# Two more batches normalized head pair by head pair, and a new order of the work

## The chip, the core and the metric

The kernel runs on one core of a Trainium2 chip. A core has a matrix engine (PE, with its weight loads shown apart as PEld), a vector engine (DVE), a scalar engine (ACT), GpSimd (POOL), and SyncE (SP), which here only issues transfers. The engines run side by side, each through its own list of instructions in order, and wait for each other through semaphores. Matmul results go to PSUM, eight banks of 512 fp32 values in each of 128 partitions; everything else lies in SBUF. The metric is the time of one execution in device microseconds.

## The reference

```python
# q, k, v: (8 batches, 8 heads, 576 tokens, 64)
kv = np.einsum('bhsd,bhse->bhde', k, v)
out = np.einsum('bhsd,bhde->bhse', q, kv)
rms = np.sqrt(np.mean(out * out, axis=-1, keepdims=True) + 1e-06)
attn = out / rms * g_norm                     # then heads side by side: x is (8, 576, 512)
h = np.maximum(x @ w_in, 0.0)                 # w_in 512 x 1024
conv = sum(conv_w[k] * hp[:, k:k + S, :] for k in range(3))   # along tokens, hp is h with a zero row at each end
y = (h * sigmoid(conv)) @ w_out               # w_out 1024 x 512
```

So there is linear attention with a norm over the 64 channels of each head and token, and then a feed-forward layer whose gate is a convolution over three neighbouring tokens. The matmuls run in bf16.

## The kernel before

A token is the smallest unit of a batch's 576 positions. Channels lie across the partitions: two heads of 64 channels make one head pair t, four pairs make the 512 channels. Batches go through the stages one after the other, several at a time, and the feed-forward part works on two batches together (pairs p = 0 to 3).

The steps have short names, and a step with its batch and part is a token of the order below:

- Lq, Lk, Lv, Li, Lo: loads of q, k, v, w_in (four quarters) and w_out, issued on POOL's queue, converted to bf16 on the way.
- kv (L358): the 64 x 64 products of k and v. kvc, kvn, ky: copies of these into SBUF; kx: the same by a transfer.
- qt, qtp (L380, L388): transposes of q on PE, with qc as copies out of PSUM; dq (L436): the same by a transposing transfer for batches 5, 6 and 7.
- ot (L430, L431): attention product of one head pair, for batches 0 to 3, one matmul of 64 columns and one of 512. oq (L464): the same for batches 4 to 7 (QUAD), as four small matmuls on quarters of the array. There the even and the odd tokens' products lie in two banks, 288 columns each, in an order with the token's residue on the outside.
- sq (L493): squares of a product on ACT, bf16, into SBUF, put in natural order of tokens. oc (L341): the product copied on ACT to SBUF as fp32 (o32).
- hm (L640): x times w_in for one slice f of 128 of the 1024 hidden channels, eight matmuls; re (L646 on ACT, L648 on DVE): its relu.
- ta, aa, ab (L682, L683, L689, L695), sg (L728), mg (L734): the convolution as scaled, shifted sums on DVE, the sigmoid on ACT, the gate on DVE. cm (L714) does a few slices of it on PE.
- om (L744): output matmuls for a tile m of 128 tokens, in eight steps or in two groups of four; ea (L341): copy out of PSUM on ACT; st (L778): the store, from SP. oh, eh, sh are the last tile in two halves.
- unread (L427): matmuls on a constant whose results nobody reads.

The squares are summed over the 64 channels of a head in one of two ways:

- In groups (`NORM`, batches 2 to 7). ss (L575) sums a batch's squares by eight matmuls into a row for each head and parity; ln (L584) takes the reciprocal root of these rows, 288 columns; sl (L591 to L594) splits it into bf16 parts on DVE, four instructions; sp (L603) spreads it back over the channels by four matmuls for each half of the tokens; mu (L629) multiplies o32 by g and by the spread factor, for two head pairs at a time. Group 2 holds batches 4 and 5, and batch 6 has group 3. Batch 7 takes its factor through DRAM (L610, L617, L625).
- Directly (batches 0 and 1). on multiplies the squares by a matrix with ones in two 64 x 64 blocks (L430, L431), which gives each channel its head's sum; nl (L542) takes the reciprocal root of 576 columns on ACT; mu0 (L562) multiplies the product, still in PSUM, by g and by the root. sqh, onh, nlh and muh (L535) are halves of these, used once.

What sets the order is a string, ORDER (lines 67 to 121 of the file): a list of tokens, written by a planner beforehand. The kernel runs through it and emits each token's instructions, and a chain of dependencies keeps each engine in the order of emission. "@n" gives a token the PSUM bank (two for a product or an hm) or the buffer of a ring, and ":1" moves a step that ACT or DVE can do to the other of the two. Thus PSUM is allocated by the string too: a step that takes a bank waits until the bank's last reader is done.

Of the kernel before, what the change touches and what calls it, by code (L numbers as in the profile page):

```python
# [54 lines left out]
AL = mybir.AluOpType  # L55
PSUM = bass.MemoryType.PSUM

NORM = {8: [2], 1: [3], 2: [4, 5], 3: [6], 4: [7]}
SPLIT = (0, 3)
QD = (5, 6, 7)  # L60
QP = (4,)
# [3 lines left out]


ORDER = """
pre@0,0,0 unread.10@0 qt0.0.0@0 ps pn qc0.0.0:1@0 pi ca.k.0 ca.v.0 kv.0.0.1@1 kvc.0.0.1.0:1@0 kvc.0.0.1.1 al.h0@0
ct@2 pg qt0.0.1@3 Lq.1.0@1 qc0.0.1:1 ot.0.0@0 Li.1 pc dg.6:1 sq.0.0@0 Li.3 unread.3@4 kv.0.1.1@3 kvc.0.1.1.0:1
dg.7:1 kvc.0.1.1.1:1 al.h1@1 Lv.1.0@1 al.x0@0 on.0.0@4 nl.0.0@0 mu0.0.0 Lk.1.0@1 Li.0 al.x1@1 unread.1@6 qt0.0.2@2  # L70
ot.0.1@6 sq.0.1@1 Lq.1.2 unread.3@3 kv.0.2.1@3 kvc.0.2.1.0:1 on.0.1@4 qt0.0.3@0 kvc.0.2.1.1:1 qc0.0.2:1@1 nl.0.1@1
mu0.0.1 ot.0.2@2 unread.3@1 kv.0.3.1@1,4 Lv.1.2 sq.0.2@2 qc0.0.3:1 kvc.0.3.1.0:1 kvc.0.3.1.1 on.0.2@6 ot.0.3@4
nl.0.2@2 mu0.0.2 sqh.0.3.0@3 unread.3@0 onh.0.3.0@6 sqh.0.3.1 nlh.0.3.0@3 onh.0.3.1 qt.1.0@2 nlh.0.3.1 qc.1.0:1@2
muh.0.3.0 muh.0.3.1 hm.0.2@6 re.0.2 hm.0.3@4 hm.0.6@6 re.0.3 ta.0.2@0 pl re.0.6 Lk.1.2 ta.0.3 aa.0.1 hm.0.7@4
re.0.7:1 cm.0.6@6 kv.1.0.2@2 kvc.1.0.2.0:1@1 sg.0.6@1 Lq.2.0@0 cm.0.7@4 kvc.1.0.2.1 Lv.2.0@0 ot.1.0@2 sg.0.7
hm.0.1@6 sq.1.0@4 qt.1.1@4 ab.0.1 on.1.0@0 nl.1.0@4 Lk.2.0@0 re.0.1:1 hm.0.0@6 re.0.0 qc.1.1@3 mg.0.3 mu0.1.0
ot.1.1@4 sq.1.1@5 kv.1.2.2@0 ta.0.0@1 kvc.1.2.2.0 kvc.1.2.2.1 on.1.1@2 nl.1.1@5 Li.2 ta.0.1 ot.1.2@0 Lq.3.0@1
ot.1.3@6 Lv.3.0@1 Lk.3.0@1 sq.1.2@6 aa.0.0 sq.1.3@7 mu0.1.1 ab.0.0 unread.1@2 on.1.2@2 nl.1.2@6 on.1.3@4 nl.1.3@7
sg.0.1 sg.0.0 qt.2.1@2 qt.2.0@4 mu0.1.2 mu0.1.3 hm.1.2@0 hm.1.3@6 re.1.2 qc.2.0@4 qc.2.1@0 mg.0.0 ta.1.2@1 hm.1.1@2
hm.1.6@0 re.1.3 kv.2.0.4@6 ta.1.3 aa.1.1 hm.0.5@4 ab.1.1 sg.0.2 re.1.1 sg.0.3 re.1.6 kvc.2.0.4.0@0 sg.1.3  # L80
kvc.2.0.4.1:1 mg.0.1 Lo.0 hm.0.4@0 ot.2.2@6 re.0.5 Lo.1 re.0.4:1 sg.1.2 mg.1.1 ta.0.4@0 ot.2.0@4 sq.2.2@0 sq.2.0@1
ta.0.5 hm.1.7@2 hm.1.4@0 re.1.7 oc.2.2@0 aa.0.2 hm.1.5@2 ot.2.1@6 re.1.4 ta.1.4@1 ab.0.2 oc.2.0@1 Lq.4.0@0 re.1.5
sq.2.1@2 qt.3.1@0 oc.2.1 sg.0.4 sg.0.5 qt.3.0@4 hm.1.0@2 ot.2.3@6 ta.1.5 qc.3.1@1 Lq.5.0@1 unread.3@0 kv.3.0.4@0
qc.3.0@2 aa.1.2 mg.0.2 sq.2.3@3 ss.2@1 kvc.3.0.4.0:1@1 kvc.3.0.4.1:1 oc.2.3 re.1.0 ln.8@0 unread.3@4 ot.3.1@2
ot.3.2@6 ot.3.0@4 ta.1.0@0 ta.1.1 ab.1.2 sq.3.2@4 oc.3.2@2 om.0.0.0@0 om.0.1.0@1 om.0.3.0@6 sq.3.0@5 oc.3.0@3
ot.3.3@4 aa.1.0 sl.8@0 om.0.1.4 sq.3.1@6 ab.1.0 om.0.3.4 oc.3.1 Lk.4.0@0 sq.3.3@7 oc.3.3 sp.2.1@2,4 ea.0.1@0
Lv.4.0@0 ea.0.3@1 mu.2.1.0 dq.5.0@3 ss.3@7 Lv.5.0@1 ln.1@0 om.0.0.4 mu.2.1.1 sp.2.0@6,2 om.0.2.0@1 qtp.4.1@4
mu.2.0.0 sg.1.5 ea.0.0@2 mu.2.0.1 hm.2.7@6 sg.1.4 om.0.2.4 qc.4.1@4 re.2.7 ea.0.2@3 sg.1.0 sg.1.1 sl.1@0 hm.2.2@4
sp.3.0@0,6 mg.1.2 mu.3.0.1 hm.2.5@2 mu.3.0.0 mg.1.0 re.2.2 cm.1.6@6 re.2.5 cm.1.7@0 dq.5.1@0 sg.1.6@1 hm.2.4@2
sg.1.7 sp.3.1@0,6 kv.4.0.4@4 mg.1.3 re.2.4 kvn.4.0.4 qtp.4.0@2 mu.3.1.0 Lk.5.0@1 ky.4.0.4.0 ky.4.0.4.1 mu.3.1.1  # L90
qc.4.0@2 hm.3.4@0 al.x2@0 hm.3.5@6 oq.4.0@2 re.3.4 re.3.5 ta.2.4@0 oq.4.1@0 hm.2.6@4 ta.2.5 sq.4.0@0 oc.4.0@1
hm.3.3@6 hm.3.6@2 re.2.6 sq.4.1@1 re.3.3 Lk.7.0@0 oc.4.1 Lv.7.0@0 hm.3.7@4 hm.3.1@0 re.3.6 aa.2.2 re.3.7 ab.2.2
om.0.6.0@4 hm.3.2@2 sg.2.5 re.3.1 sg.2.4 ta.2.6@1 ta.2.7 Lq.7.0@0 om.0.6.4 oq.4.3@0 oq.4.2@6 kv.5.0.4@5 re.3.2
aa.2.3 ea.0.6@4 Lk.6.0@1 ab.2.3 hm.2.3@2 Lv.6.0@1 sq.4.2@2 om.0.4.0@4 kvn.5.0.4:1 ky.5.0.4.0:1 ky.5.0.4.1:1 sq.4.3@3
oc.4.2@0 oq.5.0@6 oc.4.3 re.2.3 oq.5.1@0 sq.5.0@4 mg.2.2 sq.5.1@5 om.0.8.0@5 om.0.4.4 oc.5.0@3 st.0.0 ss.4@2 oc.5.1
oq.5.3@6 ea.0.4@5 oq.5.2@0 ta.2.2@0 sq.5.3@6 sq.5.2@7 om.0.8.4 ta.2.3 om.0.5.0@4 ss.5 om.0.5.4 ln.2@0 hm.2.0@2
oc.5.2@2 oc.5.3 ea.0.5@6 re.2.0 dq.7.0@1 hm.2.1@0 aa.2.1 ea.0.8@7 ab.2.1 re.2.1 sl.2@0 sp.4.1@6,2 mu.4.1.1 mu.4.1.0
om.0.7.0@4 sp.4.0@0,2 kv.7.0.4@5 mu.4.0.0 om.0.7.4 mu.4.0.1 sg.2.3 sp.5.0@0,6 sg.2.2 kvn.7.0.4:1 ea.0.7@2 mu.5.0.1
hm.3.0@2 mu.5.0.0 kx.7.0.4.0 re.3.0 al.x3@1 hm.4.4@6 al.h2@0 re.4.4 mg.2.1 sp.5.1@4,0 mu.5.1.0 kx.7.0.4.1 mu.5.1.1
hm.4.3@2 hm.4.2@6 ta.2.0@0 sg.2.7 hm.5.3@4 sg.2.6 re.4.2 hm.5.2@0 re.5.3 re.4.3 ta.2.1 oq.7.0@6 re.5.2 sq.7.0@0  # L100
oc.7.0@1 kv.6.0.4@4 oq.7.1@0 hm.5.1@2 sq.7.1@1 oc.7.1 mg.2.3 aa.2.0 kvn.6.0.4:1 hm.4.5@6 re.5.1 re.4.5 ab.2.0
hm.5.0@0 sg.2.0 sg.2.1 ta.3.2@1 re.5.0 Lq.6.0@1 ta.3.3 hm.5.5@6 hm.4.7@2 aa.3.1 re.4.7 hm.4.0@4 re.4.0 hm.4.1@0
hm.5.6@4 re.5.5 ab.3.1 mg.2.0 re.4.1 dq.7.1@2 st.0.4 kx.6.0.4.0 hm.5.4@6 om.1.5.0@0 ta.3.0@0 sg.3.2 sg.3.3 st.0.6
st.0.3 re.5.4 oq.7.3@2 re.5.6 oq.7.2@6 sq.7.3@2 kx.6.0.4.1 om.1.8.0@1 dq.6.0@4 dq.6.1@3 ta.3.1 st.0.5 sq.7.2@3
st.0.2 st.0.1 ea.1.5@5 oc.7.2@0 ss.7@4 om.1.4.0@0 hm.5.7@6 ln.4@0 oc.7.3 oq.6.0@2 oq.6.2@4 ea.1.4@4 ea.1.8@1 mg.3.1
sq.6.0@4 fw.4 fr.7.0@0 st.1.4 aa.3.0 re.5.7 oc.6.0@3 ta.3.4@1 sq.6.2@5 om.1.6.0@0 oc.6.2@2 oq.6.3@6 oq.6.1@2
om.1.7.0@1 sq.6.1@6 ta.3.5 ab.3.0 sq.6.3@7 aa.3.2 ab.3.2 ss.6@4 oc.6.3 ln.3@0 sl.3@0 oc.6.1 ea.1.7@6 om.1.0.0@5
om.1.2.0@1 mu.7.0.1 mu.7.0.0 sg.3.0 sg.3.1 sp.6.0@2,6 mu.6.0.0 mu.6.0.1 fr.7.1@1 mg.3.0 om.1.3.0@4 st.0.7 st.1.7
ea.1.2@3 hm.4.6@6 ea.1.3@0 om.1.1.0@4 ea.1.6@4 re.4.6 ea.1.0@2 mu.7.1.0 sp.6.1@6,0 mu.7.1.1 ta.3.6@0 mu.6.1.1 sg.3.5
ta.3.7 al.h3@1 hm.7.3@2 mu.6.1.0 ea.1.1@6 hm.7.7@4 hm.7.6@0 sg.3.4 aa.3.3 hm.6.2@6 re.7.3 re.7.7 hm.6.6@4 re.7.6  # L110
mg.3.2 re.6.2 re.6.6 ab.3.3 hm.6.7@6 re.6.7 hm.7.4@4 hm.7.2@6 hm.6.0@0 sg.3.6 hm.6.3@2 sg.3.7 ta.4.6@1 ta.4.7 re.7.2
re.6.0 st.1.5 st.1.2 hm.6.1@6 re.6.3 re.7.4 re.6.1 st.1.6 aa.4.3 hm.7.1@2 mg.3.3 re.7.1 ab.4.3 sg.4.7 hm.6.4@4
hm.7.5@2 st.1.1 hm.7.0@6 hm.6.5@0 sg.4.6 re.6.4 re.7.0 st.1.3 re.7.5 om.2.4.0@4 re.6.5 om.2.7.0@5 om.2.1.0@0
ta.4.2@0 ta.4.3 om.2.2.0@1 aa.4.1 ea.2.4@5 mg.4.3 ab.4.1 om.2.0.0@4 ta.4.0@1 ta.4.1 sg.4.2 om.2.5.0@2 sg.4.3 aa.4.0
mg.4.1 ab.4.0 ta.4.4@0 ea.2.7@3 ea.2.1@4 ea.2.2@6 ta.4.5 st.2.4 sg.4.1 sg.4.0 st.1.0 st.2.7 st.2.2 aa.4.2 ab.4.2
ea.2.0@0 om.2.3.0@3 ea.2.5@5 om.2.6.0@2 om.2.8.0@4 sg.4.5 mg.4.0 st.0.8 st.2.5 om.3.4.0@5 sg.4.4 mg.4.2 ea.2.6@2
ea.2.3@3 om.3.7.0@3 om.3.4.4 ea.2.8@6 st.2.1 om.3.7.4 om.3.0.0@4 om.3.3.0@2 om.3.0.4 om.3.6.0@1 om.3.5.0@0 om.3.6.4
st.2.6 st.1.8 st.2.8 ea.3.4@7 ea.3.7@5 om.3.5.4 st.2.0 st.3.4 om.3.1.0@3 st.2.3 om.3.3.4 om.3.1.4 om.3.2.0@5
ea.3.0@4 ea.3.6@2 oh.3.8.0@6 ea.3.5@1 ea.3.3@6 om.3.2.4 oh.3.8.1 ea.3.1@0 st.3.5 st.3.7 st.3.6 st.3.0 eh.3.8.0@7
ea.3.2@3 st.3.3 st.3.1 sh.3.8.0 eh.3.8.1 st.3.2 sh.3.8.1  # L120
"""


# [1 line left out]
def kernel(  # L125
# [344 lines left out]
    def product(b, t):  # L470
        ps = T["ot", b, t]
        if b in QUAD:
            return ps[:, :, :HS].rearrange("p e (r n) -> p n r e", n=PS)
        return natural(ps[:, :S])

    def in_order(b, ap):
        if b in QUAD:
            return ap.rearrange("p (n r e) -> p n r e", r=R // 2, e=2)
        return by_r(ap)
# [7 lines left out]
    @op  # L487
    def sq(b, t):
        s = T["sq", b, t] = ring("sq", [P, S], BF16, name="sq")
        if b == 0:  # L490
            nc.scalar.activation(s, T["ot", b, t][:, :S], AX.Square)
        else:
            nc.scalar.activation(in_order(b, s), product(b, t), AX.Square)  # L493
        T["sqi", b, t] = last()

    @op
# [55 lines left out]
    def x_tile(b):  # L552
        return T["x", b // 2][:, :, b % 2, :]

    @op
    def mu0(b, t):
        o, x, r = T["ot", b, t], x_tile(b)[:, t, :], T["rs0", b, t]
        if b:
            o, x, r = product(b, t), in_order(b, x), in_order(b, r)
        else:  # L560
            o = o[:, :S]
        nc.vector.scalar_tensor_tensor(x, o, g_sb, r, op0=AL.mult, op1=AL.mult)  # L562
# [266 lines left out]
```

## Time and profile before

| | |
|---|---|
| time, median of 3 runs | 179.5 us (179.39 to 180.1) |
| profiled execution | 179.07 us, span 177.3 us |
| PE busy | 170.7 us (96%), 1663 matmuls |
| ACT busy | 150.4 us (85%), of it 10 table loads of 1.28 us each |
| DVE busy | 138.4 us (78%) |
| POOL busy | 30.6 us (17%) |
| L640 (hm) | 66.4 us of PE, 512 matmuls |
| L744 (om) | 64.5 us of PE, 280 matmuls |
| L493 (sq) | 28 squares on ACT, 674 ns each |
| L341 (oc) | 24 copies to o32 on ACT, 682 ns each |
| L629 (mu) | 20 multiplications on DVE, 810 ns each |
| granted TensorE clock | full throughout |

The span is the time from the first to the last instruction that the profiler recorded. Busy time counts an instruction from its start to its end, and neighbours overlap, on PE above all, so the busy times of a group can be more than what the group adds to the span. The chain of waits is followed back from the last instruction: at each step to what released it, or else to the instruction before it on its engine; its durations run from start to start and don't overlap. A releaser is inferred from semaphores. In a group's row, "out<-in" gives the operands by the program's names, then partitions x elements, the count, the busy time in us and the mean of one in ns, and last the engine's idle time ahead of the group, with what ended it.

### The profile page before, as it was taken

The page shows a single profiled execution, that of the slowest core. Times are in us where ns is not written, and L with a number is a line of the kernel's source. Part 1 is how long each engine was busy: PE and PEld are TensorE (multiplying, and loading weights), DVE is VectorE, ACT ScalarE, POOL GpSimd, SP SyncE. Part 2 cuts the span into 40 slices and gives each one's busy share as a digit, 9 for nine tenths or more (in the row PEclk, how much of TensorE's full clock was granted, in tenths as well). Part 3 has the DMA queues.
Part 4 walks back from the last instruction along what each step waited for, and adds up shares of the span by engine and source line. Part 5 has one row for each costly group of instructions (what it writes and reads, how often), then busy time and mean ns, then how long its engine had stood idle before and what let it go on. Part 6 is the DMA issues. An engine that isn't in the chain of part 4 may idle for free.

```text
span 177.3 us, 4089 instructions
## 1 busy us (share of the span) xinstructions
PE 170.7 (96%) x1663; PEld 101.8 (57%) x1663; DVE 138.4 (78%) x235; ACT 150.4 (85%) x233; POOL 30.6 (17%) x54
## 2 busy tenths in 40 slices
PE   6999997999999999999999999999999999999993
PEld 2545763877535677653667774434577754444451
DVE  5665779889988968998799999929999999960000
ACT  2479899999999969999999999999989987782342
POOL 7997516100700031050000000000000000000000
PEclk9999999999999999999999999999999999999999
DMA  6999999999999999999995393169430004348075
GB/s 144 198 199 199 200 204 204 203 204 206 205 204 203 197 191 141 190 204 204 189 165 123 117 203 132 33 180 292 153 118 0 4 0 178 122 153 307 14 276 199
DMA packets 36219, 29.49 MB, mean 166 GB/s; under 512 B 8528, under 2 KB 31720, under 8 KB 36200
## 3 DMA queue, kind: packets, MB, share of 16 engines
q0 software_dynamic: 21760, 15.96, 59.2%
q1 hardware_dynamic: 14400, 13.26, 27.4%
q8 instruction: 13, 0.21, 0.5%
q14 instruction: 6, 0.05, 0.1%
q10 hardware_dynamic: 40, 0.01, 0.0%
HBM read 33.70 MB, written 9.58 MB: 244 GB/s over the span
## 4 chain that ended last, share of the span: by engine, by line
PE 76%; DMA 14%; POOL 5%; ACT 2%; issue 1%; POOLq 0%; ACTq 0%
PE bank L744 33%; PE bank L640 30%; DMA w_in_sb<-in_moe_w_in_dram 9%; DMA k_sb<-in_k_dram 5%; PE bank L358 2%; PE bank L464 2%; POOL q_sb L241 1%; PE bank L603 1%; PE bank L575 1%; POOL k_sb L241 1%; POOL v_sb L241 1%; PE bank L759 1%; PE bank L431 1%; PE bank L714 1%; POOL w_in_sb L315 1%
## 5 line engine op out<-in xcount | busy, mean ns | idle before, releaser
L640 PE MATMUL bank<-xT,w_in_sb 128*128 128x288 bf16 x512 | 66.4, 286 | 0.1
L744 PE MATMUL bank<-w_out_sb,h 128*128 128x512 bf16 x280 | 64.5, 379 | 0.0
L640 PEld LDWEIGHTS <-w_in_sb 128*128 128x128 bf16 x512 | 49.1, 98 | 14.7 <-issue 0.6
L744 PEld LDWEIGHTS <-h 128*128 128x128 bf16 x280 | 26.3, 98 | 30.7 <-issue 2.1
L646 ACT ACTIVATE h<-bank 128x576 bf16<-128x576 f32 x61 | 37.9, 657 | 3.1 <-PE bank L640 2.6
L728 ACT ACTIVATE taps<-taps,cwn 128x1152 bf16<-128x1152 bf16 (+1 forms) x36 | 38.0, 1093 | 1.4 <-DVE taps L695 1.3
L341 ACT ACTIVATE row<-bank 128x512 f32<-128x512 f32 (+1 forms) x37 | 21.0, 589 | 11.7 <-PE bank L744 10.0
L734 DVE TENSOR_TENSOR h<-h,taps 128x2304 bf16<-128x2304 bf16 (+1 forms) x20 | 22.3, 1114 | 3.0 <-ACT taps L728 1.8
L689 DVE TENSOR_TENSOR taps<-taps 128x2304 bf16<-128x2304 bf16 (+1 forms) x18 | 20.9, 1160 | 0.4
L695 DVE TENSOR_TENSOR taps<-taps,h 128x2304 bf16<-128x2304 bf16 (+1 forms) x18 | 20.8, 1153 | 0.2
L682 DVE TENSOR_SCALAR taps<-h,cwn 128x1152 bf16<-128x1152 bf16 (+1 forms) x36 | 17.4, 483 | 2.5 <-ACT h L646 2.4
L493 ACT ACTIVATE sq<-bank 128x576 bf16<-128x576 f32 x28 | 17.9, 674 | 0.0
L629 DVE SCALAR_TENSOR_TENSOR xT<-o,cw,bank 128x576 bf16<-128x576 f32 x20 | 15.4, 810 | 2.1 <-PE bank L603 1.9
L683 DVE TENSOR_SCALAR taps<-h,cwn 128x1152 bf16<-128x1152 bf16 (+1 forms) x36 | 16.9, 469 | 0.0
L341 ACT ACTIVATE o<-bank 128x576 f32<-128x576 f32 x24 | 16.0, 682 | 0.0
L213 ACT ACT_TABLE_LOAD x10 | 12.8, 1283 | 2.5 <-issue 2.4
L427 PE MATMUL bank<-fill 128*128 128x512 bf16 x30 | 10.1, 462 | 1.6 <-DVE fill L228 1.5
L301 POOL DMA_DIRECT2D k_sb<-in_k_dram x8 | 6.0, 750 | 26.5 <-PE bank L358 25.7
L301 POOL DMA_DIRECT2D q_sb<-in_q_dram x8 | 6.1, 760 | 17.4 <-PE bank L380 15.1
L358 PEld LDWEIGHTS <-k_sb 96*64 96x64 bf16 x384 | 7.2, 114 | 3.0 <-issue 2.4
L358 PE MATMUL bank<-v_sb,k_sb 96*64 96x64 bf16 x384 | 8.5, 199 | 0.0
L562 DVE SCALAR_TENSOR_TENSOR xT<-bank,cw,root 128x576 bf16<-128x576 f32 x7 | 5.6, 814 | 1.8 <-ACT root L542 1.7
(88 smaller groups left out, 132.0 us busy)
## 6 DMA issues: line engine op xcount, KB each, us to landing
out_dram<-row SPq DMA_DIRECT2D x35, 256.0 KB, 2.6
q_sb<-in_q_dram POOLq DMA_DIRECT2D x6, 576.0 KB, 15.0
v_sb<-in_v_dram POOLq DMA_DIRECT2D x6, 576.0 KB, 14.6
k_sb<-in_k_dram POOLq DMA_DIRECT2D x6, 576.0 KB, 14.8
factor<-factor SPq DMA_DIRECT2D x4, 288.0 KB, 4.8
w_in_sb<-in_moe_w_in_dram POOLq DMA_DIRECT2D x4, 256.0 KB, 8.5
w_out_sb<-in_moe_w_out_dram POOLq DMA_DIRECT2D x2, 512.0 KB, 19.8
q_sb<-in_q_dram POOLq DMA_DIRECT2D x4, 144.0 KB, 4.5
```

The costliest lines, as they stand in the source:

```text
L341: nc.scalar.activation(to, fr, AX.Copy)
L358: nc.tensor.matmul(ps[i][i * D:(i + 1) * D, t - t0, :], k_sb[:, 2 * t + i, r * D:(r + 1) * D], v_sb[:, 2 * t + i, r * D:(r + 1) * D], star ...
L493: nc.scalar.activation(in_order(b, s), product(b, t), AX.Square)
L640: nc.tensor.matmul(ps[:, e, :HS], w_in_sb[:, t, f * P:(f + 1) * P], x[:, t, e * HS:(e + 1) * HS], start=(t == 0), stop=(t == NT - 1))
L646: nc.scalar.activation(to, fr, AX.Relu)
L682: nc.vector.tensor_scalar_mul(tap[:, 0, f % 2, :n, 8:8 + S], h[:, f], cwn[:, 0, f:f + 1])
L683: nc.vector.tensor_scalar_mul(tap[:, 1, f % 2, :n, :S], h[:, f], cwn[:, 2, f:f + 1])
L689: nc.vector.tensor_add(tap[:, 1, :, :n, :S], tap[:, 0, :, :n, 7:7 + S], tap[:, 1, :, :n, 1:1 + S])
L695: nc.vector.tensor_add(y, y, h[:, 2 * j:2 * j + 2])
L728: nc.scalar.activation(y, y, AX.Sigmoid, scale=cwn[:, 1, f:f + 1])
L734: nc.vector.tensor_mul(h, h, T["tap", c, j][:, 1, :, :n, :S])
L744: nc.tensor.matmul(T["om", p, m], h[:, f, m * P:(m + 1) * P], w_out_sb[:, f, :], start=(f == 0), stop=(f == NF - 1))
```

## The change

Batches 5 and 6 leave the groups and are normalized directly. `DIRECT` names the batches that no group holds: 0, 1, 5 and 6.

- Their squares are no longer put in natural order: they are read and written as two contiguous halves by parity.
- on and nl (line numbers shifted) work on these squares as for batches 0 and 1, for each of four head pairs.
- mu0 gets a branch for such batches: two multiplications of 288 columns, one for each parity. The product and the root are read contiguously. The result goes to x in natural order, which means steps of six elements (12 bytes) along the inner loop of 96 and of two elements along the outer loop of three.
- So for each of the two batches ss, the copies oc, the two sp and the four mu are gone, and group 3 with its ln and sl; group 2 keeps batch 4 alone.
- The order is written anew as a whole: 690 tokens for 689. The dummy matmuls are 27 instead of 30, two relus more are done by DVE (five for three), one transposed-q copy of 1152 columns and one small copy move from DVE to ACT, and banks and ring buffers are given out anew.

```diff
-NORM = {8: [2], 1: [3], 2: [4, 5], 3: [6], 4: [7]}
+NORM = {8: [2], 1: [3], 2: [4], 4: [7]}
+DIRECT = [b for b in range(8) if b not in sum(NORM.values(), [])]
...
     def sq(b, t):
...
-            nc.scalar.activation(in_order(b, s), product(b, t), AX.Square)
+            o = product(b, t)
+            if b in DIRECT and b in QUAD:
+                s, o = s.rearrange("p (e n) -> p e n", e=2), T["ot", b, t][:, :, :HS]
+            else:
+                s = in_order(b, s)
+            nc.scalar.activation(s, o, AX.Square)
...
     def mu0(b, t):
+        if b in QUAD:
+            x = x_tile(b)[:, t, :].rearrange("p (n r e) -> p e r n", r=R // 2, e=2)
+            for e in range(2):
+                o, r = (
+                    ap.rearrange("p (r n) -> p r n", n=PS)
+                    for ap in (T["ot", b, t][:, e, :HS], T["rs0", b, t][:, e * HS:(e + 1) * HS]))
+                nc.vector.scalar_tensor_tensor(x[:, e], o, g_sb, r, op0=AL.mult, op1=AL.mult)
+            return
```

Of the order, the stretch around batch 2's sums, before and after, cut to its core (the tokens between that are not spoken of are left out as "..."):

```diff
-... hm.1.0@2 ot.2.3@6 ta.1.5 qc.3.1@1 Lq.5.0@1 unread.3@0 kv.3.0.4@0
-qc.3.0@2 aa.1.2 mg.0.2 sq.2.3@3 ss.2@1 kvc.3.0.4.0:1@1 kvc.3.0.4.1:1 oc.2.3 re.1.0 ln.8@0 unread.3@4 ot.3.1@2
-ot.3.2@6 ot.3.0@4 ... sq.3.2@4 oc.3.2@2 om.0.0.0@0 ... sq.3.0@5 oc.3.0@3
-ot.3.3@4 ... sq.3.3@7 oc.3.3 sp.2.1@2,4
+... hm.1.1@4 ot.2.3@2 ot.2.2@6 sq.2.2@2 sq.2.3@3 re.1.1 oc.2.2@1 mg.0.2 kv.3.0.4@0 ss.2@1 qt.3.0@4 qt.3.1@6
+... oc.2.3 ln.8@0 unread.1@0 ot.3.0@4
+ot.3.1@2 sq.3.0@4 oc.3.0@2 ot.3.2@6 unread.1@0 om.0.1.0@0 ... sq.3.1@5 ... oc.3.1 sq.3.2@6 ot.3.3@2
+... oc.3.2@3 sl.8@0 ... sq.3.3@7 oc.3.3 ea.0.0@0 om.0.1.4 sp.2.1@6,2
```

And the one in which batch 5 is normalized in the new order:

```diff
+oq.5.0@6 oq.5.1@2 sq.5.0@3 ... om.0.4.0@0 ... on.5.0@4 mg.2.2 ab.2.3 om.0.5.4 nl.5.0@4 om.0.4.4
+mu0.5.0 hm.2.3@4 oq.4.1@6 sq.5.1@4 ... om.0.6.0@0 re.2.3 sq.4.1@5 ... on.5.1@4
+ta.2.3 om.0.6.4 oc.4.1 aa.2.1 nl.5.1@7 ss.4@1 oq.5.3@4 ... ea.0.6@4 oq.5.2@6 mu0.5.1 ln.2@0 om.0.7.0@0 sq.5.3@6
+sq.5.2@7 sl.2@0 on.5.3@2 om.0.7.4 nl.5.3@0 mu0.5.3 ea.0.7@6 on.5.2@2 ... nl.5.2@7 om.0.8.0@1
+kv.7.0.4@0 sp.4.0@2,4 mu0.5.2 ...
```

## The prediction

> **What bounds the kernel now.** I read the shares of the page first, then the chain of waits from 36 us on, then busy time by stretch, then the groups of instructions for the prices.
>
> ```profile
> span 177.3 us, 4089 instructions
> PE 170.7 (96%) x1663; PEld 101.8 (57%) x1663; DVE 138.4 (78%) x235; ACT 150.4 (85%) x233; POOL 30.6 (17%) x54
> ```
>
> PE is the bound by share, and ACT is the only other engine near it. The shares are averages, so the chain decides. The columns are start, duration and what the time went to.
>
> ```profile
> 20.48 16.20 DMA w_in_sb<-in_moe_w_in_dram
> 36.69 0.05 issue
> 36.73 2.13 PE bank L640 x16
> ...
> 45.01 0.65 PE bank L427 x3
> 45.66 0.88 PE bank L358 x48
> 46.54 0.36 PE bank L575 x8
> ...
> 48.53 0.50 ACT rs L584
> ...
> 54.07 0.97 PE bank L744 x4
> 55.04 0.23 PE bank L603 x4
> ...
> 57.74 0.86 PE bank L744 x4
> ```
>
> Three things are to be seen. The last quarter of w_in lands at 36.69, and its first matmul starts at once: whatever is gained before that point is waited away. From there the chain is PE almost throughout until 174.2 (ACT holds it only from 48.4 to 51.2). And four output matmuls cost 0.86 when a full-array matmul follows and 0.97 when the small-tile L603 follows: a visit to small tiles (L358, L380, L464, L575, L603) costs about 0.10 on top of its work.
>
> By stretch, the columns are the stretch and its length, then PE, PEld, DVE, ACT and POOL busy:
>
> ```profile
> 36.70:53.30 16.60, 16.50 (x194) 10.00 (x194) 15.20 (x32) 16.57 (x30) 3.85 (x5) 1.00 1.29 205
> 73.00:83.00 10.00, 10.00 (x122) 5.14 (x120) 9.54 (x14) 9.98 (x18) 2.30 (x3) 1.00 1.31 209
> 83.00:93.00 10.00, 10.00 (x122) 5.95 (x122) 8.43 (x14) 9.92 (x15) 0.00 (x0) 1.00 1.20 181
> 93.00:106.00 13.00, 13.00 (x152) 10.18 (x151) 12.93 (x18) 13.00 (x20) 0.00 (x0) 1.00 0.61 142
> 106.00:120.00 14.00, 14.00 (x102) 6.22 (x100) 10.74 (x16) 13.97 (x24) 0.00 (x0) 1.00 0.42 127
> ```
>
> Batch 5 is normalized between 73 and 93 and batch 6 between 106 and 130. ACT has no idle time to speak of in either; only after 140 does it have some (16.2 of 20 us, then 5.5 of 17.3). So PE sets the end, with ACT half a step behind it.
>
> **The prices**, from the groups by shape (busy, mean ns):
>
> ```profile
> L493 ACT ACTIVATE sq<-bank 128x576 bf16<-128x576 f32 x28 | 17.9, 674 | 0.0
> L341 ACT ACTIVATE o<-bank 128x576 f32<-128x576 f32 x24 | 16.0, 682 | 0.0
> L542 ACT ACTIVATE root<-bank,eps_sb 128x576 f32<-128x576 f32 x7 | 5.2, 742 | 0.7 <-PE bank L431 0.5
> L629 DVE SCALAR_TENSOR_TENSOR xT<-o,cw,bank 128x576 bf16<-128x576 f32 x20 | 15.4, 810 | 2.1 <-PE bank L603 1.9
> L562 DVE SCALAR_TENSOR_TENSOR xT<-bank,cw,root 128x576 bf16<-128x576 f32 x7 | 5.6, 814 | 1.8 <-ACT root L542 1.7
> L535 DVE SCALAR_TENSOR_TENSOR xT<-bank,cw,root 128x288 bf16<-128x288 f32 x2 | 0.9, 514 | 0.4 <-ACT root L528 0.4
> ```
>
> Neighbours on a queue overlap: squares and copies follow each other at 0.54 (chain: 49.03, 49.57, 50.11), a root of 576 columns is followed after 0.64 (timeline: 14.15 to 14.79), two multiplications of 576 start 0.73 apart, so one of 288 takes 0.43 to 0.51.
>
> **The change, part by part.**
>
> *PE work after 36.73.* Gone: two L575 groups (0.36 each) and four L603 groups (0.23 each), 1.64 together, and four of the six dummy matmuls that lay there (6 to 2, 0.22 each), 0.86. Added: eight pairs of matmuls with ones, each 0.24 as the product pairs of the same shapes in the chain, 1.94. Net −0.56. Before 36.73 the two batch 1 round trips also get shorter, by about 0.2 by my sums; I count that at nothing, since the loads queued ahead of the last w_in quarter are the same ones in both orders and it should land at 36.7 again. If POOL issued it later, the whole would move one for one.
>
> *Visits to small tiles after 36.73.* Counted in the two orders: 24 before, 18 after, at 0.10 each: −0.6.
>
> *Waits of PE.* Here the new order pays. Just after batch 2's products it has one kv (0.88) and no dummies ahead of ss.2, which needs the last square. From the start of ot.2.2: product 0.24, about 0.2 to the square's start, squares 0.53 and 0.67, release 0.07, so 1.71; PE gets there after 0.24 + 0.88 = 1.12. It waits about 0.6, and the dummies taken out here are no gain. ACT then sets the pace over the squares and copies of batch 3: I sum 1.35 of waits up to sp.2.1, where before had 0.35. So sp.2.1 starts at 53.3 in both, with 0.3 more PE work left in the new order. Later: about 0.2 where sp.3.1 waits for the parts of L591 to L594; about 0.35 in batch 5, mostly at the ones products: on.5.2 takes the bank that nl.5.3 reads, PE covers that with 0.25 + 0.86 = 1.11, the root needs 0.25 + 0.22 + 0.74 + 0.05 = 1.26; 0.2 elsewhere and at the last piece. That is 0.75 against 0.45 before. All waits: 2.1 against 0.8, +1.3.
>
> *ACT.* Eight copies to o32 go (−8 × 0.54 = −4.3), eight roots come (+8 × 0.64 = 5.1), one root of 288 columns goes (−0.4), two relus go to DVE (−1.1), a transposed-q copy of 1152 columns (1.1) and a small copy (0.2) come. Net +0.6 to +0.9 for an engine that was full from 73 to 130. The table loads stay at ten. What covers it is the distance between ACT's results and PE's use of them: by the two orders laid over the row times, results that came up to 3 us ahead in the old order come 0.8 to 1.4 us ahead in the new one. I take it as just covered; uncovered it costs up to 0.9 and more through the round trips (first rival).
>
> *DVE.* Eight L629 (−8 × 0.73 = −5.8) and one set of parts (−1.5) go; sixteen multiplications of 288 (16 × 0.43 = 6.9) and two relus (+1.4) come, 0.9 of copies leave. About zero. It is never on the chain after 36.7. The first users of batch 5's result are matmuls of hm.5.3 far behind; the nearest wait is oq.4.1 for the bank that mu0.5.0 frees: PE has 2.7 us of work there, the trip takes 2.2 (ones 0.25, 0.2 to the root's start, root 0.74, 0.05, two multiplications 0.95).
>
> *The new multiplication's writes.* It reads PSUM and root contiguously and writes bf16 every 12 bytes. No row of before has such a write. Strided reads of PSUM cost nothing (L562 reads strided, 814; L629 does not, 810), so the lower bound is the row, 0.43 to 0.51; as upper bound I take twice the row, as if it made one access per element where L535 makes one per two. I take the row, the nearest; the upper end is a rival. The Trainium skill, "SBUF — State Buffer", Specifications, says that a line holds 16 bytes and that full bandwidth needs two hits per line; 12-byte steps give 1.33, so by that page the writes would be slowed. No run here shows it yet.
>
> *Queues and end.* SP loses nothing and gains nothing in bytes; the q transposes and the stores are reissued in other places, with their first users over 1 us behind. At the end the last piece, its copy (0.38) and its store stay as they were, but two more stores lie in the last 2 us: 0 to +0.3, I take +0.15.
>
> **Sum.** −0.56 − 0.6 + 1.3 + 0.15 = +0.3 us, against an execution whose span was 177.3 and whose time was 179.07, so 1.8 us lie around the span. The median of the runs is 179.5, 0.4 above that execution; the forecast stands on the median: 179.8 us. This kernel's runs spread over 0.7 us, so about 0.5% (0.9 us) is what can be told from no change.
>
> **Rivals.**
>
> *ACT becomes the bound between 73 and 130 us: slower.* Against it: the results still lead by 0.8 us by my sums. For it: the stretches above show ACT at 9.9 to 10 of 10, and ones product and root of one head pair follow its square directly on ACT, so ACT idles for up to a product (0.25 + 0.2) in each of the four trips of batch 5, which the page would show as L542 waiting for L431. It decides once ACT's delay passes 0.8 us. Price: 0.9 more work and four times 0.4 of idle, 2.5, less the 0.8 of lead: +1.7. PE's savings then count for nothing, so it stands on the old median: 181.2.
>
> *The writes at 12-byte steps take double: slower.* Sixteen times 0.43 is 6.9 us more on DVE. In 73 to 93 it had 0.46 + 1.57 idle for 3.5 more, so 1.5 us of delay enter the stretch to 106, where DVE is full (12.93 of 13); batch 6's 3.5 meet 3.3 idle, 0.2 over. If what waits on DVE has no slack, 1.7 reach PE: 179.8 + 1.7 = 181.5. At oq.4.1 the trip would be 3.1 for 2.7. Against it: nothing but the nearest row. By the rule of the Trainium skill given above, on that page of SBUF lines, this would be the outcome.
>
> *PE's waits don't appear: faster.* If ACT runs half a step earlier at ss.2, as it did before (results there were 0.9 ahead), PE keeps −0.56 − 0.6 and the waits stay at 0.8: 179.5 − 1.2 = 178.3. Against it: the wait at ss.2 is a sum of four rows in a fixed order.
>
> **How the numbers follow.** The balance has 0.45 (179.8, own range 178.9 to 180.4), ACT as bound 0.25 (181.2), the slow writes 0.10 (181.5), no waits 0.20 (178.3). Only the last is below 178.6, so faster 0.20; the two slower ones make 0.35; the rest 0.45. The range for 8 in 10 reaches from 178.2, which holds the faster case, to 181.6, which takes in both slow ones at their price and leaves out what is worse.
>
> **What would show it.** After: PE near 170 busy, chain still PE from 36.7; the dummies of L427 (now L428) fall from 30 to 27, the pairs with ones rise by eight; a PE wait of 0.5 or more near 46 us for the squares on ACT; the new multiplication at 0.43 to 0.55 (0.9 or more if the writes are slow). The prediction is wrong if w_in lands away from 36.7, if ACT's idle ahead of the roots of 576 columns passes 1 us in batch 5, or if no PE wait shows near 46.

## The result and the profile after

The changed kernel takes 185.9 us (185.57 to 186.75) for 179.5 before: 1.036 times as long (95% interval 1.0315 to 1.0399), 6.4 us slower. The forecast was 179.8 us with a range up to 181.6. The profiled execution took 186.75 us, the longest of its four, with a span of 185.0. (One execution of a kernel tried below took 594 us, with PE busy for 588 of them; nothing is read from it.)

The page of the changed kernel, its first part:

```profile
span 185.0 us, 4050 instructions
PE 173.7 (94%) x1644; PEld 103.9 (56%) x1644; DVE 146.9 (79%) x239; ACT 151.5 (82%) x232; POOL 31.4 (17%) x54
```

DVE has gained 8.5 us of work where the forecast had none. The groups by shape say where (the multiplication of batches 5 and 6 is L569, the old direct one is L576 now):

```profile
L569 DVE SCALAR_TENSOR_TENSOR xT<-bank,cw,root 128x288 bf16<-128x288 f32 x16 | 16.9, 1225 | 1.6 <-ACT root L548 1.5
L576 DVE SCALAR_TENSOR_TENSOR xT<-bank,cw,root 128x576 bf16<-128x576 f32 x7 | 5.6, 815 | 3.5 <-ACT root L548 3.4
```

Half as many columns take one and a half times as long: 1225 ns for 288 columns, 815 for 576. The nearest row of before, L535, had 514 for the same 288 columns. The chain of waits of the changed kernel, from batch 5 on:

```profile
79.05 1.27 DVE taps L709
80.32 2.05 DVE xT L569 x2
...
85.33 2.06 DVE xT L569 x2
...
88.97 3.99 DVE xT L569 x4
...
93.01 1.02 PE bank L654 x7
...
120.89 2.15 DVE xT L569 x2
...
124.22 2.06 DVE xT L569 x2
```

Before, DVE was never on the chain after 36.7 us. Now it holds it from 75 to 93 and again at 121 and 124, and six pairs of the new multiplication lie on it with 12.3 us. What waits for them is PE, in the view of waits (engine and line, what it waited for, us, times, longest):

```profile
PE bank L465 <- DVE xT L569: 2.2, 4, 0.7
PE bank L654 <- DVE xT L569: 1.4, 2, 0.7
PEld L431 <- DVE xT L569: 1.4, 1, 1.4
PE bank L431 <- DVE xT L569: 0.9, 1, 0.9
```

Products (L465), a hidden slice (L654) and a ones product (L431) wait for a bank whose product the multiplication reads: 4.5 us. The 1.4 us of the weight load (PEld) are the same wait as the 0.9 of L431, seen from the other side, and don't count twice. By stretch, PE then stands idle where it had been full (columns as before: length, then PE, PEld, DVE, ACT, POOL):

```profile
73.00:83.00 10.00, 9.13 (x108) 5.19 (x106) 9.56 (x13) 9.03 (x14) 2.29 (x3) 1.00 1.31 210
83.00:93.00 10.00, 7.75 (x95) 3.34 (x93) 9.86 (x15) 8.28 (x12) 0.00 (x0) 1.00 1.27 212
120.00:140.00 20.00, 18.64 (x115) 10.51 (x114) 18.23 (x21) 16.64 (x24) 0.00 (x0) 1.00 0.54 160
```

### The profile page after: what moved, and what is told of

The parts are those of the page before. It is cut to its first block, busy times and chain, and to the rows that moved or that the text cites. A ratio compares the mean times of both kernels' runs of the same rounds, so it can differ in the third digit from the quotient of the medians.

```text
span 185.0 us, 4050 instructions
## 1 busy us (share of the span) xinstructions
PE 173.7 (94%) x1644; PEld 103.9 (56%) x1644; DVE 146.9 (79%) x239; ACT 151.5 (82%) x232; POOL 31.4 (17%) x54
## 4 chain that ended last, share of the span: by engine, by line
PE 66%; ACT 14%; DVE 12%; DMA 3%; issue 3%; POOLq 0%
PE bank L654 27%; PE bank L758 26%; DVE xT L569 7%; ACT sq L499 3%; ACT taps L742 3%; ACT h L660 3%; DMA q_sb<-in_q_dram 3%; PE bank L359 2%; PE bank L428 2%; ACT o L342 2%; PE bank L728 2%; ACT root L548 2%; PE bank L381 2%; DVE taps L703 1%; PE bank L432 1%
## 5 line engine op out<-in xcount | busy, mean ns | idle before, releaser
L654 PE MATMUL bank<-xT,w_in_sb 128*128 128x288 bf16 x512 | 66.1, 286 | 1.4 <-DVE xT L569 1.4
L654 PEld LDWEIGHTS <-w_in_sb 128*128 128x128 bf16 x512 | 49.2, 98 | 16.2 <-issue 2.6
L660 ACT ACTIVATE h<-bank 128x576 bf16<-128x576 f32 x59 | 37.0, 671 | 2.7 <-PE bank L654 2.5
L748 DVE TENSOR_TENSOR h<-h,taps 128x2304 bf16<-128x2304 bf16 (+1 forms) x20 | 22.2, 1112 | 2.9 <-ACT taps L742 2.3
L696 DVE TENSOR_SCALAR taps<-h,cwn 128x1152 bf16<-128x1152 bf16 (+1 forms) x36 | 16.8, 467 | 2.5 <-ACT h L660 2.5
L569 DVE SCALAR_TENSOR_TENSOR xT<-bank,cw,root 128x288 bf16<-128x288 f32 x16 | 16.9, 1225 | 1.6 <-ACT root L548 1.5
L697 DVE TENSOR_SCALAR taps<-h,cwn 128x1152 bf16<-128x1152 bf16 (+1 forms) x36 | 16.6, 462 | 0.0
L548 ACT ACTIVATE root<-bank,eps_sb 128x576 f32<-128x576 f32 x15 | 11.0, 739 | 4.4 <-PE bank L432 4.3
L342 ACT ACTIVATE o<-bank 128x576 f32<-128x576 f32 x16 | 10.8, 690 | 0.0
L643 DVE SCALAR_TENSOR_TENSOR xT<-o,cw,bank 128x576 bf16<-128x576 f32 x12 | 9.2, 806 | 1.2 <-PE bank L617 1.2
L302 POOL DMA_DIRECT2D k_sb<-in_k_dram x8 | 6.8, 851 | 14.6 <-PE bank L359 13.8
```

Source lines behind the costliest of these rows:

```text
L342: nc.scalar.activation(to, fr, AX.Copy)
L569: nc.vector.scalar_tensor_tensor(x[:, e], o, g_sb, r, op0=AL.mult, op1=AL.mult)
L654: nc.tensor.matmul(ps[:, e, :HS], w_in_sb[:, t, f * P:(f + 1) * P], x[:, t, e * HS:(e + 1) * HS], start=(t == 0), stop=(t == NT - 1))
L660: nc.scalar.activation(to, fr, AX.Relu)
L696: nc.vector.tensor_scalar_mul(tap[:, 0, f % 2, :n, 8:8 + S], h[:, f], cwn[:, 0, f:f + 1])
L697: nc.vector.tensor_scalar_mul(tap[:, 1, f % 2, :n, :S], h[:, f], cwn[:, 2, f:f + 1])
```

## The experiments

Theory 1 was the rival of the prediction: the writes at 12-byte steps. Theory 2 was that the new order is slow by itself, with ACT as the bound.

**The multiplication with other steps.** The first run has the squares in natural order again and one even step of 4 bytes in the write:

```diff
-            o = product(b, t)
-            if b in DIRECT and b in QUAD:
-                s, o = s.rearrange("p (e n) -> p e n", e=2), T["ot", b, t][:, :, :HS]
...
+            nc.scalar.activation(in_order(b, s), product(b, t), AX.Square)
...
-            x = x_tile(b)[:, t, :].rearrange("p (n r e) -> p e r n", r=R // 2, e=2)
+            x = x_tile(b)[:, t, :].rearrange("p (n r e) -> p e n r", r=R // 2, e=2)
+            w = T["rs0", b, t].rearrange("p (n r e) -> p e n r", r=R // 2, e=2)
```

> The changed kernel, with its order, in which squares of batches 5 and 6 go back to natural order (strided read of PSUM, contiguous write) and the two multiplications per head pair write x at one even step of 4 bytes instead of nested steps of 12; root read at 8-byte steps, product strided from PSUM. Theory 1 (the 12-byte writes are the cause): each multiplication takes 0.5 us instead of 1.23, the PE waits at oq.4.1, the last hm and om of that stretch, oq.6.0 and oq.6.1 (6.5 us together) go, time about 179.5 to 180.5. Rival (the new order is slow in itself, ACT the bound): multiplications get fast but PE then waits for ACT roots, time 182 to 185.

The second exchanges the loops alone:

```diff
-            x = x_tile(b)[:, t, :].rearrange("p (n r e) -> p e r n", r=R // 2, e=2)
+            x = x_tile(b)[:, t, :].rearrange("p (n r e) -> p e n r", r=R // 2, e=2)
...
-                    ap.rearrange("p (r n) -> p r n", n=PS)
+                    ap.rearrange("p (r n) -> p n r", n=PS)
```

> The changed kernel with only the two loops of the multiplication exchanged: writes go at 4-byte steps in sequence, but now the fp32 root in SBUF is read at 384-byte steps (and the product in PSUM as well). If only the write's step counts, 0.5 us each and the same time as with the natural order, 179.5 to 180.5. If an SBUF read at far steps costs as the write does, about 1 to 1.2 us each and the time stays at 184 to 186.

Both are 1.0056 times before (intervals 1.0034 to 1.0078 and 1.0031 to 1.0082), 180.5 and 180.7 us. The group and the waits of the second:

```profile
L569 DVE SCALAR_TENSOR_TENSOR xT<-bank,cw,root 128x288 bf16<-128x288 f32 x16 | 8.0, 541 | 3.0 <-ACT root L548 2.9
```

```profile
PEld L431 <- DVE xT L569: 0.4, 1, 0.4
```

The multiplication falls from 1225 to 541 ns with the same operands, engines and order, and PE's waits for it from 4.5 us to none (the 0.4 left is a weight load's, and no matmul waits with it). Some 5.4 of the 6.4 us are the order of two loops (1.0357 against 1.0056 of before).

The changed kernel and this one issue the same 1644 matmuls in the same order, so the starts of the matmuls can be compared one by one. After the first matmul behind w_in the changed kernel falls behind at six places: 1.15 us at oq.4.1, 0.92 at on.5.3, 0.30 at the spread sp.4.0, 1.38 at hm.3.1, 1.11 at oq.6.0 and 0.91 at oq.6.1, 5.8 us together. Nowhere else does one matmul lose more than 0.08.

Where the root is read, at 8-byte or at 384-byte steps, makes no difference (537 and 541 ns). About 1.0 us is left with the order; it is taken up below.

**The steps by themselves.** The kernel before, with a series behind its work:

```diff
+    stt = lambda o, a, c: nc.vector.scalar_tensor_tensor(o, a, g_sb, c, op0=AL.mult, op1=AL.mult)
+    for k in (1, 2, 3, 4, 5, 6, 8, 12):          # elements between writes
+        for _ in range(3):
+            stt(every(bo, k), flat, flat)
...
+            nc.scalar.activation(every(bo, k), flat, AX.Copy)
```

> The kernel before, with a series of 288-column multiplications and ACT copies on dead SBUF buffers added behind its work (their time is in the span and is left out): bf16 written at steps of 2, 4, 6, 8, 10, 12, 16 and 24 bytes, the two loop orders, fp32 written at 4 to 16 bytes, fp32 read at 8 to 32 bytes, and the same writes by ACT. Theory 1 as a rule of two hits per 16-byte line: flat at 0.5 us up to 8 bytes, rising beyond, with 12 bytes at 1.0 to 1.2. Rival (PSUM operands or contention with PE make the multiplication slow in the changed kernel): 12 bytes stay near 0.5 here, where all operands lie in SBUF and the other engines are idle.

Groups by line of this run, each for the stretch of one pattern (three instructions; busy us, mean ns): bf16 writes at steps of 2, 4, 8, 12 and 16 bytes, then the changed kernel's nested loops, then the exchanged ones:

```profile
L797 DVE SCALAR_TENSOR_TENSOR w_in_sb<-taps,cw 128x288 bf16<-128x288 f32 x3 | 1.6, 519 | 0.2
L797 DVE SCALAR_TENSOR_TENSOR w_in_sb<-taps,cw 128x288 bf16<-128x288 f32 x3 | 1.6, 543 | 0.1
L797 DVE SCALAR_TENSOR_TENSOR w_in_sb<-taps,cw 128x288 bf16<-128x288 f32 x3 | 2.6, 860 | 0.1
L797 DVE SCALAR_TENSOR_TENSOR w_in_sb<-taps,cw 128x288 bf16<-128x288 f32 x3 | 3.5, 1175 | 0.2
L797 DVE SCALAR_TENSOR_TENSOR w_in_sb<-taps,cw 128x288 bf16<-128x288 f32 x3 | 4.5, 1492 | 0.1
L797 DVE SCALAR_TENSOR_TENSOR w_in_sb<-taps,cw 128x288 bf16<-128x288 f32 x3 | 3.5, 1174 | 0.1
L797 DVE SCALAR_TENSOR_TENSOR w_in_sb<-taps,cw 128x288 bf16<-128x288 f32 x3 | 1.7, 554 | 0.1
```

All operands lie in SBUF here. PE still runs the last output matmuls under the steps of 2 to 10 bytes (it ends at 174.8 us), but from the second write at 12 bytes on it is idle, and the nested loops, from 186.9 us on, take 1174 ns all the same. So neither PSUM nor contention with PE is needed to make them slow. The whole series, mean ns of 288 columns by the trace's records:

| step in bytes | 2 | 4 | 6 | 8 | 10 | 12 | 16 | 24 |
|---|---|---|---|---|---|---|---|---|
| DVE writes bf16 | 519 | 543 | 702 | 860 | 1024 | 1175 | 1492 | 1481 |
| ACT writes bf16 | 442 | 523 | | 837 | | 1157 | 1473 | 1466 |
| DVE writes fp32 | | 516 | | 519 | | 602 | 727 | |
| DVE reads fp32 | | | | 511 | | 593 | 719 | |

From 6 to 16 bytes the bf16 write grows with the stretch that it covers, and then it stays. At 8 bytes 288 elements cover 144 lines of 16 bytes, at 16 bytes 288: (1492 − 860) / 144 = 4.4 ns for each further line. By that, 12 bytes (216 lines) should take 1176, and it takes 1175. The rule of the Trainium skill, "SBUF — State Buffer", Specifications, that two hits on a 16-byte line are needed for full bandwidth, holds for fp32 (519 at 8 bytes, 727 at 16). For bf16 writes the chip is stricter than the rule: with two hits on a line, at 8 bytes, the time is already 860.

**One batch at a time.** Exchanged loops for one batch, 12-byte writes for the other:

```diff
+                if b == 6:                       # 5 in the counterpart
+                    y, o, r = (ap.rearrange("p n r -> p r n") for ap in (x[:, e], o, r))
```

> The changed kernel with the loops exchanged for batch 5 only; batch 6 keeps the 12-byte writes. Theory (each PE wait is local: the bank that a slow multiplication frees late): the waits at oq.6.0 and oq.6.1, 2.05 us in the changed kernel, stay as they are and those of batch 5 go; time 180.6 + 2.0 = 182.7. Rival (DVE falls behind as a whole, and batch 6's waits are batch 5's delay carried on): batch 6 has DVE idle of its own, waits shrink below 1 us, time under 181.5.

> The counterpart: 12-byte writes for batch 5 only, exchanged loops for batch 6. In the changed kernel PE waited 4.3 us more in batch 5 than with the exchanged loops (at the last hm of batch 2, oq.4.1, the output matmuls around the roots, the spread of batch 4). If the waits are local and add up: 180.6 + 4.3 = 184.9, less what small waits they absorb, so 184.0 to 184.9, and together with batch 6 alone (+1.7) the whole 5.2 to 6. Rival (both share one backlog): the sum of the two is well off the whole, 183 or less.

Batch 6 alone: 1.0156 (1.0125 to 1.0187), 182.3 us. Batch 5 alone: 1.0283 (1.0231 to 1.0336), 184.9 us. Above the version with all loops exchanged that is 1.0% and 2.3%, together 3.3% for the 3.0% of the changed kernel: the waits are local and add up. Two of the four executions with batch 5 slow (185.58 and 185.34 us) had a mean granted clock of 0.991, the other two (184.19 and 184.49) 1.000, as the changed kernel had in all four; by these two batch 5 costs some 2.1%, and the sum is 3.1%. The view of waits with batch 6 slow:

```profile
PE bank L465 <- DVE xT L573: 1.3, 2, 0.7
```

and with batch 5 slow:

```profile
PE bank L658 <- DVE xT L573: 1.4, 2, 0.7
PEld L431 <- DVE xT L573: 1.4, 1, 1.4
PE bank L465 <- DVE xT L573: 0.9, 2, 0.7
PE bank L431 <- DVE xT L573: 0.9, 1, 0.9
```

With batch 6 slow, PE falls behind the version with exchanged loops by 1.11 us at oq.6.0 and 0.90 at oq.6.1, as in the changed kernel (1.11 and 0.91), with no backlog from batch 5 and idle time on DVE close by (1.3 of 5 us from 113 to 118): idle elsewhere doesn't help a product that waits for this bank now. (The views of waits show less, since they count from the modelled end of the matmul before.)

**The wait at ss.2.** In the version with exchanged loops, the sigmoid sg.0.5 and its gate mg.0.2 are put behind the squares, and the two squares change places:

```diff
-... sg.0.4 Lo.1 sg.0.5 hm.1.1@4 ot.2.3@2 ot.2.2@6 sq.2.2@2 sq.2.3@3 re.1.1 oc.2.2@1 mg.0.2 kv.3.0.4@0 ...
+... sg.0.4 Lo.1 hm.1.1@4 ot.2.3@2 ot.2.2@6 sq.2.3@3 sq.2.2@2 re.1.1 oc.2.2@1 sg.0.5 kv.3.0.4@0 ...
-... qt.3.1@6 aa.1.2 kvc.3.0.4.0:1@1 ...
+... qt.3.1@6 aa.1.2 mg.0.2 kvc.3.0.4.0:1@1 ...
```

> The changed kernel with exchanged loops, and in the order the second sigmoid of the pair ahead of batch 2's squares moved behind them (its gate on DVE likewise), so that the squares come 0.7 us earlier for the PE wait at ss.2 of 0.72. If that wait is a loss of its own: time 180.6 - 0.7 = 179.9. Rival (ACT sets the pace over the whole stretch up to the first spread, so PE waits later instead): sp.2.1 starts at the same time as without the move, within 0.2, and the time stays at 180.4 to 180.8.

> The same kernel as the move of the second sigmoid (184.0 us, 3.3 more than without the move), for its profile, since the profile taken then was of an execution of 594 us. Theory (the move only shifted the wait): PE waits under 0.3 at ss.2 and more than 3 us at the first output matmuls, which need the gate that comes later. Rival: the waits lie elsewhere, behind sp.2.1.

It got slower, 1.024 (1.0204 to 1.0276), 183.8 us without the execution of 594. The chain of the same kernel in the second of these runs, 184.3 us:

```profile
46.32 0.67 ACT taps L742
...
47.01 0.76 DVE h L748
47.77 0.33 DVE kvbd L344
...
48.65 0.68 DVE qT L344
...
49.59 0.43 PE bank L432
```

The wait at ss.2 fell from 0.72 to 0.41 us, but the gate (L748) now stands late in DVE's queue, and behind it the copies of kv and q for batch 3: PE waits 1.6 and 0.4 us for them, and the first spread starts at 56.70 for 54.15. The rival was nearest, but the wait didn't just move, it grew. Another thing is to be seen: after these waits the 512-column matmul takes 0.43 us for the usual 0.22. The granted clock, the third number from the end, says why:

```profile
50.00:51.00 1.00, 1.00 (x6) 0.36 (x4) 1.00 (x3) 0.99 (x3) 1.00 (x2) 0.50 1.29 208
53.00:54.00 1.00, 1.00 (x6) 0.48 (x5) 0.97 (x3) 1.00 (x3) 0.00 (x0) 1.00 1.32 206
```

It is 0.50 from 49.3 to 52.8 us. At half speed these 3.4 us cost 1.7 us of PE's work, an estimate from this trace and about half of the whole loss. All five executions of the first run at about 184 us have a mean clock of 0.990 to 0.991 as well, where this one has 0.990.

**One part alone, put by hand into the old order.** Batch 6 direct, all the rest as before; first with the exchanged loops, then with the 12-byte writes:

```diff
-NORM = {8: [2], 1: [3], 2: [4, 5], 3: [6], 4: [7]}
+NORM = {8: [2], 1: [3], 2: [4, 5], 4: [7]}
...
+... om.1.6.0@0 on.6.0@6 nl.6.0@0 mu0.6.0 om.1.7.0@1 on.6.2@6 oq.6.3@2 nl.6.2@3 mu0.6.2 sq.6.3@7 ta.3.5 ab.3.0 ea.1.6@4
+om.1.0.0@0 oq.6.1@4 on.6.3@6 sq.6.1@6 nl.6.3@0 mu0.6.3 ... om.1.2.0@1 on.6.1@6 nl.6.1@3 mu0.6.1 ...
```

> One part alone: the order of before with batch 6 alone normalized directly, with 4-byte writes, its tokens put by hand into the stretch where batch 6 was normalized before. By rows: PE work +0.15 (ones 0.97, sums and spreads -0.82), three visits to small tiles less (-0.3), ACT about 0, DVE -1.0. Theory (direct normalization is worth next to nothing by itself): 179.5 plus or minus 0.5. Rival (a direct batch waits at its ones products and roots, and the new order's extra 1 us is of that kind): 180.3 or more, with PE idle ahead of the ones products.

> The kernel with batch 6 alone direct in the old order, but with the changed kernel's 12-byte writes. Against the 4-byte version each of the eight multiplications takes 0.65 to 0.7 us longer on DVE (5.4 us in all). If such a loss always reaches PE through the bank: +1.5 to +2.5 over the 4-byte version. If DVE's idle in that stretch (3.3 us between 106 and 120) and the order hide it: less than +0.7.

> Batch 6 alone direct in the old order, as in the run before, but with the copies out of PSUM (ea.1.6 and three others) given row buffers whose last store is done: in that run ACT waited at ea.1.6 for a store that stood behind the factor transfers on SP, and PE waited 3.8 us at that place and 10 in all. If that was the whole of it: 179.5 to 180.5 us. If direct trips put by hand cost by themselves: PE still waits ahead of the ones products, 181 or more.

They took 1.0566 (1.0531 to 1.0601), 1.0607 (1.0561 to 1.0652) and, with other row buffers, 1.0366 (1.0331 to 1.04) of before. None says what a direct batch is worth, because my placing cost more than anything it was to measure. The last one's chain:

```profile
119.50 0.27 ACT root L548
...
120.14 0.64 ACT sq L499
120.78 0.49 ACT row L342
...
121.32 1.89 PE bank L758 x8
123.21 0.28 PE bank L465 x4
...
123.51 0.35 ACT sq L499
...
124.05 0.73 ACT root L548
124.79 0.50 ACT row L342
...
125.33 1.89 PE bank L758 x8
```

Each output matmul waits for a row copy on ACT that stands behind a square and a root, and these stand behind the output matmul before: the trips run one after another instead of beside other work. That the stores explained the first run is only partly so: 3.4 of 10 us. A part of the 3.4 can be the clock's: in the first run it is 0.50 for 3.4 us from 122.8 us on, after PE had done nothing from 120 to 122, and all six executions have a mean clock of 0.982 to 0.991; of the last run only one in six has a clock so low (0.991, at 187.5 us the slowest). Between the first two the 12-byte writes cost 0.4%, with overlapping intervals, under waits that hide them; it decides nothing.

## Why the prediction was wrong

The failed step is "The new multiplication's writes", where I took the nearest row as the price, "0.43 to 0.51", and "twice the row" as the upper bound. The measured price is 1.23 us in the kernel and 1.17 alone, above that bound: not one access per element against one per two, but 4.4 ns for each 16 bytes of destination. L535 writes contiguously and was no row for this. I had noted that by the Trainium skill, "SBUF — State Buffer", Specifications, the writes would be slowed, and this was the right warning; I gave the case 0.10.

The rival of the slow writes had the right cause and too small a price, 181.5. The double that it took, 0.86 for one multiplication, is short of the 1.03 measured from start to start (2.05 for a pair). Above all it set DVE's extra time against DVE's idle time by stretch. The runs show that idle time hides nothing here: each pair's bank is needed by PE at one moment, and PE lost time at six such places. I had worked one of them out, oq.4.1 (a trip of 3.1 for 2.7, so 0.4), and it measured 1.15: in DVE's queue the pair stood behind two sums of the convolution and a gate, of which the lines above show the last (79.05) and the pair itself (80.32 to 82.37).

The rest of the sum can be judged on the version with exchanged loops, where the forecast was +0.3 us and the measured difference +1.0 (0.6 to 1.5), just past the 180.4 where the balance's own range ends. What follows compares one trace with one trace, so it is argued and not tested. The four pieces add up to 1.7 us, by which the two profiled spans differ (179.0 and 177.3), and 0.6 of it is the first:

- The anchor. "It should land at 36.7 again" is right for the transfer (36.6), but its first matmul came at 37.3. This is hardly the change: in the five profiled executions of the old order at that place it came at 36.7 to 37.9 and in the six of the new one at 37.1 to 37.8, and before's, at 36.7, was the earliest.
- The wait at ss.2 was forecast as 0.6 and is 0.72, and ACT paces PE up to the first spread as said: from the anchor to there 16.8 us for 16.65, where I had the same time for both.

The chain of the version with exchanged loops at the first spread (L617) and at the output matmuls ahead of the second:

```profile
54.15 0.34 PE bank L617 x4
...
54.85 0.97 PE bank L758 x4
```

- The visits to small tiles cost what I said (0.97 ahead of a spread here as before), but the small waits around them are larger: from the first spread to the last copy 121.7 us for 121.2, forecast +0.1.
- The end: the stores in the last microseconds take 3.1 us from the last copy for 2.7, forecast +0.15, upper bound 0.3.
- That ACT is the bound between 73 and 130 did not come: with the loops exchanged PE is full there (9.96 of 10 us from 83 to 93, 20.0 of 20 from 120 to 140), and ACT has no idle time ahead of batch 5's roots (0.9 us in the changed kernel, under the 1 us that I had named as a sign).

The rival without waits is wrong too: the wait at ss.2 is there, at 0.72 us, in every run that keeps the new order at that place. The forecast's own sum is thus 0.7 us short, and the writes are the other 5.4.

## What to carry to other kernels

When an access pattern has no row in the trace, the nearest row by size is not its price: look at the step between consecutive elements of the innermost loop, and choose the loop order that writes bf16 at 2 or 4 bytes, also where the reads then go far. Idle time of an engine in a stretch says little about whether it can be slower there; ask for each instruction which bank it frees and when the next user comes. In a hand-ordered schedule a step that depends on another engine's late result delays everything queued behind it, so a wait of 0.7 us that looks free to take away can cost 3, here by the estimate above about half of it through a halved clock. Look at the granted clock by stretch behind every new wait of PE.

## What was unexpected of the hardware

- A bf16 write costs 4.4 ns per 16 bytes covered once its step passes 4 bytes, up to a step of 16, on DVE and ACT alike (860 and 837 ns at 8 bytes, 1175 and 1157 at 12), where an fp32 write at the same 8 bytes is free (519).
- Reads at 384-byte steps with three of them in turn, as in the exchanged loops, cost 554 ns, less than the 719 of an even 16-byte step.
- After waits of 1.6 and 0.4 us PE ran at half its clock for 3.4 us (granted clock 0.50, 0.43 us for a 512-column matmul). With batch 5 alone slow it did so too, from 93.1 us on, after waits of 0.2 to 0.9 us within the 13 us before. The changed kernel had these same waits and kept its clock, so the length of the waits alone doesn't decide it; what does is open. The Trainium skill, "TensorE: Matmul & The Clock Gate", Part 1, gives about 3.4 us as the idle window after which the clock is halved; here less was enough.
